# A slab opening with five tiles, a norm multiply moved to VectorE, and the order of the last waits

## The chip, the cores and the metric

The kernel runs on one core of a Trainium2 chip. The metric is the device time of one launch in microseconds (us). Several launches are timed and the median is taken.

## What is computed

The reference chains a linear attention and a feed-forward layer. Batch is 8, with 8 heads, 576 positions and a head dimension of 64; the layer is 512 to 2048 to 512.

```
q_s = softmax(q, over the head dimension)
k_s = softmax(k, over the sequence)
kv  = k_s^T v                      # 64 x 64 per batch and head
x   = q_s kv                       # laid out as 4608 tokens x 512
h   = x @ w_in                     # 4608 x 2048
g   = h * sigmoid(beta * h)
out = g @ w_out                    # 4608 x 512, float32
```

## The kernel before, in words

The output is made in nine slabs. Slab t (0 to 7) holds the first 512 positions of batch t; slab 8 holds the 64 positions that each batch has left over. The work on TensorE (PE) is one long list of matmuls:

- The **first pass** of a slab makes 16 tiles of 128 hidden features (function `pass1_mm`, L406 in the profile through the helper `mm`). A tile takes four matmuls of 512 columns, one for each part m of the 512 inputs (XT parts 0 to 3), summed in a bank of PSUM. ScalarE (ACT) then applies Silu (L746) and VectorE (DVE) scales the result (L769) into GT. The banks are HB (0, 1, 2) in turn; the fourth tile takes bank 3. The first three tiles are opened together, m by m, in the order of `LEAD`, so that XT parts 2 and 3 are wanted only after six matmuls.
- The **second pass** (`pass2_fast`, L846) multiplies by w_out as seven products of 16 matmuls of 256 columns, in the manner of Strassen: it works on sums (GS1, GS2, WSUM) and on differences of halves of GT, which `g_diff` makes in place on VectorE (L812). The products use one HB bank and the two OB banks 3 and 4. Product four is copied out of bank 3 by ScalarE, product five out of bank 4 by ScalarE (`copy`, L882), and products six and seven are added to TS by VectorE (`last`, L894) into O2S. Product seven uses bank 4 again, so it waits for the copy of product five.
- The **attention** for the next batches is laid between these matmuls. ScalarE takes the exponentials (L319). `norm_main` normalises q: VectorE sums (reduce L357) and inverts (L359), and then a multiply in place (L361) follows, for half a batch (two head pairs, 128x1024) on GpSimd (POOL). `turn` transposes that half by a DMA from SyncE's (SP) queue (L606) into QT. `kv_all` makes keys times values on PE (L482); VectorE scales it into KVD (L490, L459). `quad` multiplies KVD by QT on PE (L554); VectorE casts the even parts to XT and ScalarE the odd ones (L596). For slabs 2 and 3, part 0 and 1 (first half) are made late in the second pass before, part 2 and 3 (second half) within the opening of the slab itself. `cast_v` and `cast_vr` put v into bf16 on GpSimd (L377, L391).

The order is written out by hand in two ways. `tick` counts slots of PE (64 in a first pass, 64 in a second) and runs an entry of `todo` when its slot comes; `hooks` run at named places of the second pass (hook 3 ahead of product four, 4 ahead of five, 5 ahead of six, 6 ahead of seven). Each engine has one queue, in the order in which the program adds its instructions. Waits are put in by `Program.plan` from what an instruction reads and writes; `after` adds a further one.

`silu_table` is a tiny Silu activation (L1054) that makes ScalarE load the Silu table before it is wanted. `load` issues the loads of a batch from SP (three of 1 MB, for even batches four of the remaining rows as well). `store` sends a finished slab out from SP. At the end SP waits for all stores (L151).

Second pass t below is that of slab t: in second pass 1 the attention of batch 2 is made, in second pass 2 that of batch 3, and the exponentials of q of batch 4 as well.

Of the kernel before, what the change touches and what calls it, by code (L numbers as in the profile page):

```python
# [18 lines left out]
NF = DFF // 128  # L19
NM = DM // 128  # L20
NG = NF // 2
# [23 lines left out]
class Program:  # L45
# [83 lines left out]
    def emit(self, nc, es):  # L129
        counts, waits = self.plan()  # L130
        sems = {}
        for key in counts:
            sems[key] = es.enter_context(nc.semaphore("s_" + "_".join(str(x) for x in key)))
        by = {e: [] for e in (PE, ACTE, DVE, POOL, SP)}
        for op, w in zip(self.ops, waits):
            by[op.eng].append((op, w))

        def run(eng):
            def body(h):
                for op, w in by[eng]:  # L140
                    for key, n in w:
                        h.wait_ge(sems[key], n)
                    ins = op.fn(h)
                    if op.slot is not None:
                        ins.then_inc(sems[op.count[0]], 16)
                    elif op.inc:
                        ins.then_inc(sems[op.count[0]], 1)
                if eng == SP:
                    for key, n in sorted(counts.items(), key=str):
                        if key[0] == "dma" and str(key[1]).startswith("out"):  # L150
                            h.wait_ge(sems[key], n)  # L151
            return body

        with nc.Block() as blk:
            for e in (PE, ACTE, DVE, POOL, SP):
                getattr(blk, e)(run(e))


def bass_efficient_attn_shen__then__act_swish_beta_kernel(
# [12 lines left out]
    with ExitStack() as es:  # L172
# [48 lines left out]
        HB = (0, 1, 2)  # L221
        OB = (3, 4)
        MB = (5, 6, 7)

        P = Program()
# [376 lines left out]
        def turn(b, hp0, n):  # L602
            i = b % 2
            o = bass.AP(QT[i], hp0 * 512, [[2048, 128], [128, 4 * n], [1, 128]])
            a = bass.AP(EQ[i], hp0 * 512, [[2048, 128], [1, 512 * n]])
            add(SP, lambda e: e.dma_start_transpose(o, a),  # L606
                r=[("eq", i, hp) for hp in range(hp0, hp0 + n)],
                w=[("qt", i, hp) for hp in range(hp0, hp0 + n)], slot=f"tq{i}{hp0}")
# [6 lines left out]
        def norm_turn(b, hp0):  # L615
            norm_main(b, hp0, 2, POOL)
            turn(b, hp0, 2)

        def norm_turn_rem():
            norm_rem()  # L620
            turn_rem()

        def one(fn, *a):
            return lambda: fn(*a)

        def steps(fn, *a):
            return lambda: go(fn(*a))
# [8 lines left out]
        def attn_late(b):  # L636
            if b < 4:
                x = 100 if b == 2 else 97
                return [(x, steps(kv_all, b)), (x + .1, lambda: g_diff(1)),
                        (118, one(quad, b, (0,)))]  # L640
            return [(96, steps(kv_all, b)), (99, lambda: g_diff(1)), (112, one(quad, b))]

# [95 lines left out]
        hrot = [0]  # L738
# [16 lines left out]
                pass1_mm(t, f, m, bk)  # L755
                tick()

        LEAD = tuple((n, m) for m in range(NM) for n in range(3))

        def pass1_lead(t, fs, tick):  # L760
            bks = [HB[(hrot[0] + n) % 3] for n in range(3)]
            hrot[0] += 3
            for n, m in LEAD:
                pass1_mm(t, fs[n], m, bks[n])
                tick()

# [43 lines left out]
        def g_diff(fh):  # L810
            f, th = NG * fh, 1 - fh
            add(DVE, lambda e: e.tensor_tensor(gv(f, th, NG), gv(f, th, NG), gv(f, 1 - th, NG),  # L812
                                               ALU.subtract),
                r=gk(f, 0, NG) + gk(f, 1, NG), w=gk(f, th, NG), war=True)
# [140 lines left out]
        for t in range(NSLAB):  # L955
            todo = []
            if t == 0:
                todo = [(x, steps(t_steps, 1, (hp,), NOW, ACTE))
                        for hp, x in enumerate((97, 106, 114, 119))]
                todo += [(107, one(exp_kr_s, 1))]  # L960
                todo += [(x, one(exp_k, 1, hp, 1)) for hp, x in enumerate((108, 115, 120, 125.5))]
                todo += [(x, one(cast_v, 1, hp, DVE))
                         for hp, x in ((1, 118.5), (2, 123), (3, 127))]
                todo += [(x, steps(kv_steps, 1, (hp,), NOW))
                         for hp, x in enumerate((118, 122, 126))]
                todo += [(x, steps(out_step, 1, hp, NOW, ACTE)) for hp, x in enumerate((122.5, 125))]
                todo += [(117, one(o2_evac, 0, 0, 3, ACTE))]
                todo += [(2, steps(out_step, 0, 3, HEAD, DVE))]
            elif t < 4:
                todo = attn_late(t + 1)  # L970
                if t > 1:
                    todo += [(1.5, one(quad, t, (1,)))]
                if t == 3:
                    todo += [(4, one(norm_turn, 4, 2))]
                if t == 1:
                    todo += [(1, steps(out_step, 1, 2, (3,), ACTE)),
                             (3, steps(kv_steps, 1, (3,), (7,))),
                             (6, steps(out_step, 1, 3, (7,), DVE)),
                             (6.1, one(w_sum, 2, 4, 4)), (6.2, one(w_diff, 0)),
                             (6.3, one(w_diff, 1))]  # L980
            elif t < 7:
                todo = attn(t + 1)
            elif t == 7:
                todo = spread(outr_steps(1), 32, 48)
            todo = sorted(todo, key=lambda x: -x[0])
# [7 lines left out]
            def ftile(n):  # L993
                return n if t == 0 else n // 2 + NG * (n % 2)

            for n in range(NF + 1):
                if n == 0:
                    pass1_lead(t, [ftile(x) for x in range(3)], tick)
                elif 2 < n < NF:
                    pass1_tile(t, ftile(n), tick, 3 if n == 3 else None)  # L1000
                if n:
                    scale_g(ftile(n - 1))
                    for i_, w_ in {8: ((0, 4),), 12: ((4, 2),), 14: ((6, 1),), 16: ((7, 1),)}.get(
                            n if t else 0, ()):
                        g_sum1(i_, w_)
                        g_sum2(i_, w_)
                    if t == 2 and n == 2:
                        for hp in range(NHP):
                            cast_v(3, hp, after=P.writer[("gt", 0, 0)])
                if t == 0 and n == 14:  # L1010
                    w_sum(1)
                if t == 1 and n in (4, 7, 10):
                    o2_evac(0, n // 3, 3 + n // 3, ACTE)
                    if n == 10:
                        store(0)
# [28 lines left out]
            def on(n, fn, *a):  # L1044
                hooks.setdefault(n, []).append(lambda: fn(*a))
# [8 lines left out]
                add(ACTE, lambda e: e.activation(DUMMY[:, 2:3], WARM[:, 0:1], ACT.Silu),  # L1054
                    r=["warm"], w=["dummy"])

            def casts(b):
                g = P.writer[("gs2", NG - 1)]
                if b % 2 == 0:
                    cast_vr(b, after=g)  # L1060
                for hp in range(NHP):
                    cast_v(b, hp, after=g)

            if t == 1:
                on(0, exps, 2)
                on(0, casts, 2)
                on(2, norm_turn, 2, 0)
                on(3, norm_turn, 2, 2)
                on(3, g_diff, 0)
                on(4, silu_table)  # L1070
                on(3, load, 4)
            elif t == 2:
                on(0, exps, 3)
                on(2, norm_turn, 3, 0)
                on(3, norm_turn, 3, 2)
                on(3, g_diff, 0)
                on(3, load, 5)
                on(4, exp_q, 4)
                on(4, silu_table)
                on(4, casts, 4)  # L1080
                on(6, norm_turn, 4, 0)
            elif t == 3:
                on(0, exp_k, 4)
                on(0, exp_kr, 4)
                on(0, exp_q, 5)
                on(3, g_diff, 0)
                on(4, norm_turn, 5, 0)
                on(5, norm_turn, 5, 2)
                on(4, exp_qr, 1)
                on(5, exp_k, 5)  # L1090
                on(5, norm_turn_rem)
                on(5, casts, 5)
                on(5, load, 6)
                on(7, load_rem, "qrf", qt_h, QRF, 4)
            elif t + 2 < B:
                b = t + 2
                on(0, exps, b)
                on(0, casts, b)
                if t == 4:
                    on(0, load, 7)  # L1100
                on(3, norm_turn, b, 0)
                on(4, norm_turn, b, 2)
# [40 lines left out]
```

The softmax here doesn't subtract the row's maximum and nothing guards it: scores larger than these inputs give would overflow.

## Time and profile before

| What | Value |
|---|---|
| Median of 8 runs | 272.96 us (272.35 to 274.28) |
| The profiled execution | 272.75 us, of which span 270.9 us |
| TensorE matmuls | busy 264.1 us (97%), granted clock 0.998 |
| VectorE | busy 192.5 us (71%) |
| ScalarE | busy 181.3 us (67%) |
| GpSimd | busy 63.0 us (23%) |
| Second pass 1, slab 2 first pass | 60.65 to 74.67, 74.67 to 89.11 us |
| Second pass 2, slab 3 first pass | 89.11 to 103.69, 103.69 to 118.12 us |

The span is the time between the first and the last instruction in the profile; the rest of the execution's time lies around it. A matmul's record is longer than the distance to the next one, since they are pipelined: the start of a 512-column matmul comes 0.216 us after that of the one before it, the start of a 256-column one 0.109 us. In the profile's lines "DVE", "ACT", "POOL" and "SP" are VectorE, ScalarE, GpSimd and SyncE; "PEld" is TensorE's load of weights, and a "q" after a name is the engine's own queue of instructions, as for DMAs that it issues. A timeline line has the start, the duration, the engine, the line of code, the operation, its output and input, how many there were in a row, and in brackets the idle time before and what ended it.

### The profile page before, as it was taken

Reading aid. Unit: us, or ns where it says so; the run is one execution under the profiler, and the core shown is the slowest. Engines: PE = TensorE matmul, PEld = TensorE weight load, DVE = VectorE, ACT = ScalarE, POOL = GpSimd, SP = SyncE. Lnnn points to the kernel's source line nnn. Section 1 sums busy time; section 2 is a strip of 40 time slices with the busy share of each in tenths; the row PEclk is TensorE's granted clock in tenths of the full one; section 3 lists DMA queues with packets and bytes.
Section 4 is the critical chain, followed back from the end, with each engine's and each line's share of the span. In section 5 each row is a group of like instructions: output and inputs, shape, how many; then the busy total and the mean of one; then the engine's idle time right before and its main releaser. Section 6 shows DMA issues by size and latency. Waiting matters only on the chain.

```text
span 270.9 us, 5010 instructions
## 1 busy us (share of the span) xinstructions
PE 264.1 (97%) x1993; PEld 163.6 (60%) x1993; DVE 192.5 (71%) x407; ACT 181.3 (67%) x289; POOL 63.0 (23%) x80
## 2 busy tenths in 40 slices
PE   8999999999999999999999999999999999999994
PEld 2444444448744875478645864587458745874683
DVE  4964586887967798868778876887588448626762
ACT  4898658789468974887778937893883387018610
POOL 2790010006530089000910660036000100000000
PEclk9999999999999999999999999999999999999999
DMA  7999999989799129940499999503600130012005
GB/s 216 320 204 207 226 324 349 297 222 374 179 329 302 64 53 293 279 156 2 80 284 275 287 354 154 163 8 73 213 2 0 41 135 2 0 70 87 0 2 156
DMA packets 59367, 45.95 MB, mean 170 GB/s; under 512 B 28608, under 2 KB 58320, under 8 KB 58320
## 3 DMA queue, kind: packets, MB, share of 16 engines
q1 hardware_dynamic: 54480, 40.90, 53.7%
q0 software_dynamic: 4240, 4.19, 9.4%
q10 hardware_dynamic: 624, 0.53, 0.6%
q8 instruction: 16, 0.26, 0.4%
q14 instruction: 7, 0.06, 0.1%
HBM read 36.71 MB, written 9.44 MB: 170 GB/s over the span
## 4 chain that ended last, share of the span: by engine, by line
PE 84%; DVE 4%; DMA 3%; ACT 2%; POOL 2%; SPq 2%; issue 1%; POOLq 0%
PE PS L406 50%; PE PS L846 31%; DMA VF<-in_v_dram 2%; PE PS L482 1%; PE PS L554 1%; DMA QT<-EQ 1%; POOL VB L377 1%; DVE QS L357 1%; SPq L278 1%; SPq L290 1%; ACT EQ L319 1%; DVE EQ L361 1%; POOL EQ L361 1%; DVE VB L377 1%; ACT GT L746 1%
## 5 line engine op out<-in xcount | busy, mean ns | idle before, releaser
L406 PE MATMUL PS<-XT,WIN 128*128 128x512 bf16 x576 | 127.8, 380 | 0.1
L746 ACT ACTIVATE GT<-PS,BETA 128x512 bf16<-128x512 f32 x144 | 95.2, 689 | 39.5 <-PE PS L406 39.3
L406 PEld LDWEIGHTS PS<-XT,WIN 128*128 128x128 bf16 x576 | 55.0, 98 | 64.8 <-DVE XT L596 0.7
L769 DVE TENSOR_SCALAR GT<-GT,RB 128x512 bf16<-128x512 bf16 x144 | 52.5, 386 | 38.7 <-ACT GT L746 37.9
L361 POOL TENSOR_TENSOR EQ<-EQ,QI 128x1024 bf16<-128x1024 bf16 (+1 forms) x13 | 25.6, 1966 | 48.8 <-DVE QI L359 48.1
L846 PE MATMUL PS<-WSUM,GT 128*128 128x256 bf16 x256 | 30.1, 273 | 1.0 <-ACT O2S L882 1.0
L846 PE MATMUL PS<-WOUT,GS 128*128 128x256 bf16 x256 | 31.1, 273 | 0.0
L846 PE MATMUL PS<-WOUT,GT 128*128 128x256 bf16 x256 | 29.8, 273 | 0.0
L846 PEld LDWEIGHTS PS<-WSUM,GT 128*128 128x128 bf16 x256 | 24.8, 98 | 5.0 <-ACT O2S L882 1.2
L882 ACT COPY O2S<-PS 128x512 f32<-128x512 f32 (+1 forms) x17 | 9.4, 559 | 26.1 <-PE PS L846 26.1
L846 PEld LDWEIGHTS PS<-WOUT,GT 128*128 128x128 bf16 x256 | 24.8, 98 | 3.0
L846 PEld LDWEIGHTS PS<-WOUT,GS 128*128 128x128 bf16 x256 | 24.8, 98 | 3.0
L319 ACT ACTIVATE EQ<-QF 128x512 bf16<-128x512 f32 x32 | 17.9, 620 | 7.4 <-DMA QF<-in_q_dram 7.3
L805 DVE TENSOR_TENSOR GS<-GT 128x512 bf16<-128x512 bf16 (+2 forms) x32 | 21.9, 685 | 0.0
L812 DVE TENSOR_TENSOR GT<-GT 128x2048 bf16<-128x2048 bf16 x16 | 21.6, 1374 | 0.0
L377 POOL CAST VB<-VF 128x512 bf16<-128x512 f32 x24 | 15.6, 650 | 22.1 <-DVE GS L805 13.4
L357 DVE TENSOR_REDUCE QS<-EQ 128x16 f32<-128x1024 bf16 (+1 forms) x20 | 19.7, 984 | 0.9 <-ACT EQ L319 0.9
L319 ACT ACTIVATE EK<-KF 128x512 bf16<-128x512 f32 x32 | 18.1, 620 | 0.1
L894 DVE TENSOR_TENSOR O2S<-TS,PS 128x512 f32<-128x512 f32 (+1 forms) x17 | 10.8, 647 | 9.7 <-PE PS L846 9.7
L846 PE MATMUL PS<-WSUM,GS 128*128 128x256 bf16 x128 | 16.6, 273 | 0.0
L406 PE MATMUL PS<-WOUT,GT 128*128 128x512 bf16 x64 | 15.5, 380 | 0.0
L846 PEld LDWEIGHTS PS<-WSUM,GS 128*128 128x128 bf16 x128 | 12.5, 98 | 3.2
(90 smaller groups left out, 209.4 us busy)
## 6 DMA issues: line engine op xcount, KB each, us to landing
out_dram<-O2S SPq DMA_DIRECT2D x8, 1024.0 KB, 4.9
QF<-in_q_dram SPq DMA_DIRECT2D x6, 1024.0 KB, 7.0
KF<-in_k_dram SPq DMA_DIRECT2D x6, 1024.0 KB, 9.4
VF<-in_v_dram SPq DMA_DIRECT2D x6, 1024.0 KB, 12.2
KF<-in_k_dram SPq DMA_DIRECT2D x8, 256.0 KB, 5.5
VF<-in_v_dram SPq DMA_DIRECT2D x8, 256.0 KB, 5.5
WOUT<-in_moe_w_out_dram POOLq DMA_DIRECT2D x4, 512.0 KB, 16.4
WIN<-in_moe_w_in_dram POOLq DMA_DIRECT2D x3, 512.0 KB, 9.1
```

The source lines that it names most:

```text
L319: add(ACTE, lambda e, o=o, a=a: e.activation(o, a, ACT.Exp), r=[(name + "f", i, hp)], w=[("e" + name, i, hp)])
L357: add(DVE, lambda e: e.tensor_reduce(s_, a, AX.X, ALU.add), r=ks, w=[("qs", i, hp0)])
L361: add(eng, lambda e: e.tensor_tensor(a, a, vb, ALU.mult), r=ks + [("qi", i, hp0)], w=ks)
L377: add(eng, lambda e: (e.copy if eng == ACTE else e.tensor_copy)(o, a), r=[("vf", i, hp), ("vone", i)], w=[("vb", i, hp)], after=after)
L406: add(PE, lambda e: e.matmul(o, l, r_, start=start, stop=stop), r=r, w=w, bank=[bk])
L746: add(ACTE, lambda e: e.activation(GT[:, f, :], PS[bk][:, :], ACT.Silu, scale=BETA[:, f:f + 1]), r=[("ps", bk), "beta"], w=[("gt", f, 0), ...
L769: add(DVE, lambda e: e.tensor_scalar(GT[:, f, :], GT[:, f, :], RB[:, f:f + 1], None, ALU.mult), r=k + ["rb"], w=k)
L805: add(DVE, lambda e: e.tensor_tensor(GS2[:, i:i + n, :], GT[:, i:i + n, :], GT[:, i + NG:i + NG + n, :], ALU.add), r=[k_ for f in (i, i + ...
L812: add(DVE, lambda e: e.tensor_tensor(gv(f, th, NG), gv(f, th, NG), gv(f, 1 - th, NG), ALU.subtract), r=gk(f, 0, NG) + gk(f, 1, NG), w=gk(f ...
L846: add(PE, lambda e, l=l, r_=r_, st=st, u=u, i=i, b_=b_: e.matmul(PS[b_][:, 256 * u:256 * u + 256], l, r_, start=st, stop=end and i == NG - ...
L882: add(eng, lambda e, b_=b_, u0=u0, u1=u1: (e.copy if eng == ACTE else e.tensor_copy)(o[:, u0:u1, :], bank3(b_)[:, u0:u1, :]), r=[("ps", b_ ...
L894: add(DVE, lambda e, b_=b_, u0=u0, u1=u1: e.tensor_tensor(o[:, u0:u1, :], ts[:, u0:u1, :], bank3(b_)[:, u0:u1, :], ALU.add), r=["ts", ("ps ...
```

## The change

Three things are changed.

1. Slabs 2 and 3 open with five tiles m by m instead of three. The fourth and fifth use the OB banks 3 and 4. Their order is m = 0 and 1 of four tiles, m = 0 and 1 of the fifth, then m = 2 and 3 of all five: parts 2 and 3 of XT are wanted after ten matmuls. The quad that makes these parts goes from tick 1.5 to tick 6.
2. For batches 2 and 3 the sums and inverses of the second half stay at hook 3, but the multiply goes from GpSimd to VectorE, after keys times values and the second difference; its transpose follows it. The difference and the multiply are one entry of `todo` (`diff_norm`). The loads of batches 4 and 5 go from hook 3 to hook 4, the casts of batch 4 wait for that multiply, and in second pass 2 the Silu table goes from hook 4 to hook 6.
3. At the end SP waits for the stores in the order of their issue instead of the order of their names.

```diff
+        last = {op.count[0]: op.pos for op in self.ops if op.slot is not None}
...
-                    for key, n in sorted(counts.items(), key=str):
-                        if key[0] == "dma" and str(key[1]).startswith("out"):
-                            h.wait_ge(sems[key], n)
+                    for key in sorted((k for k in counts if str(k[1]).startswith("out")),
+                                      key=lambda k: last[k]):
+                        h.wait_ge(sems[key], counts[key])
...
+        def diff_norm(b):
+            g_diff(1)
+            norm_main(b, 2, 2, sums=False)
+            turn(b, 2, 2)
...
-                return [(x, steps(kv_all, b)), (x + .1, lambda: g_diff(1)),
+                return [(x, steps(kv_all, b)), (x + .1, one(diff_norm, b)),
                         (118, one(quad, b, (0,)))]
...
-        LEAD = tuple((n, m) for m in range(NM) for n in range(3))
+        LEAD = {3: tuple((n, m) for m in range(NM) for n in range(3)),
+                5: tuple([(n, m) for m in range(2) for n in range(4)] + [(4, 0), (4, 1)]
+                         + [(n, m) for m in range(2, NM) for n in range(5)])}
 
         def pass1_lead(t, fs, tick):
-            bks = [HB[(hrot[0] + n) % 3] for n in range(3)]
+            bks = [HB[(hrot[0] + n) % 3] for n in range(3)] + list(OB)
             hrot[0] += 3
-            for n, m in LEAD:
+            for n, m in LEAD[len(fs)]:
...
-                    todo += [(1.5, one(quad, t, (1,)))]
+                    todo += [(6, one(quad, t, (1,)))]
                 if t == 3:
                     todo += [(4, one(norm_turn, 4, 2))]
...
+            lead = 5 if t in (2, 3) else 3
             for n in range(NF + 1):
                 if n == 0:
-                    pass1_lead(t, [ftile(x) for x in range(3)], tick)
-                elif 2 < n < NF:
+                    pass1_lead(t, [ftile(x) for x in range(lead)], tick)
+                elif lead <= n < NF:
...
+            def norm_sums(b, hp0):
+                norm_main(b, hp0, 2, mult=False)
+
-            def casts(b):
-                g = P.writer[("gs2", NG - 1)]
+            def casts(b, key=("gs2", NG - 1)):
+                g = P.writer[key]
...
             if t == 1:
...
-                on(3, norm_turn, 2, 2)
+                on(3, norm_sums, 2, 2)
                 on(3, g_diff, 0)
                 on(4, silu_table)
-                on(3, load, 4)
+                on(4, load, 4)
             elif t == 2:
...
-                on(3, norm_turn, 3, 2)
+                on(3, norm_sums, 3, 2)
                 on(3, g_diff, 0)
-                on(3, load, 5)
                 on(4, exp_q, 4)
-                on(4, silu_table)
-                on(4, casts, 4)
+                on(4, casts, 4, ("eq", 1, 2))
+                on(4, load, 5)
+                on(6, silu_table)
                 on(6, norm_turn, 4, 0)
```

## The prediction

> **What bounds the kernel now.** I read the busy shares first, then the chain that ended last, then the timeline of the two stretches that the diff touches, engine by engine, and last the waits.
>
> ```profile
> PE 264.1 (97%) x1993; PEld 163.6 (60%) x1993; DVE 192.5 (71%) x407; ACT 181.3 (67%) x289; POOL 63.0 (23%) x80
> PE 84%; DVE 4%; DMA 3%; ACT 2%; POOL 2%; SPq 2%; issue 1%; POOLq 0%
> ```
>
> TensorE is busy in 97% of the span and carries 84% of the chain. So an edit pays or costs what it adds to, or takes from, TensorE's idle gaps. The gaps lie at the end of second passes 1 and 2 and where slabs 2 and 3 open:
>
> ```profile
> 70.66 2.12 DVE L812 TENSOR_TENSOR GT<-GT 128x2048 bf16<-128x2048 bf16 x1
> 72.28 0.41 PE L554 MATMUL PS<-QT,KVD 64*64 64x512 bf16 x4 [0.24 <-DMA QT<-EQ]
> 72.62 2.21 PE L846 MATMUL PS<-WSUM,GT 128*128 128x256 bf16 x17
> 74.67 0.60 PE L406 MATMUL PS<-XT,WIN 128*128 128x512 bf16 x2
> 75.19 0.41 PE L554 MATMUL PS<-QT,KVD 64*64 64x512 bf16 x4
> ...
> 98.95 2.12 DVE L812 TENSOR_TENSOR GT<-GT 128x2048 bf16<-128x2048 bf16 x1
> 99.90 1.28 ACT L1054 ACT_TABLE_LOAD   x1
> 100.31 0.41 PE L554 MATMUL PS<-QT,KVD 64*64 64x512 bf16 x4
> 100.65 0.28 PE L846 MATMUL PS<-WSUM,GT 128*128 128x256 bf16 x1
> 101.31 0.57 ACT L882 COPY O2S<-PS 128x512 f32<-128x512 f32 x1
> 101.93 0.28 PE L846 MATMUL PS<-WSUM,GT 128*128 128x256 bf16 x1 [0.99 <-ACT O2S L882]
> 102.19 1.20 DVE L357 TENSOR_REDUCE QS<-EQ 128x16 f32<-128x1024 bf16 x1
> 103.89 0.69 DVE L894 TENSOR_TENSOR O2S<-TS,PS 128x512 f32<-128x512 f32 x1 [0.21 <-PE PS L846]
> ```
>
> In second pass 2 the largest single gap shows: the last product's first matmul starts at 101.93 instead of 100.76 (100.65 plus one 256-column step of 0.109), because ScalarE's copy of its bank stands behind a table load. Slabs 2 and 3 themselves have almost no gap: from 75.54 on, matmuls follow every 0.216 us. And the last lines of the span:
>
> ```profile
> SPq L151 <- DMA out_dram<-O2S: 1.9, 1, 1.9
> L151 SPq EVENT_SEMAPHORE  x6: 17/28/1872, 268.3 to 270.5; - x6
> ```
>
> SyncE's second of six waits takes 1.87 us and ends at 270.26, when the last output has landed; the other four follow, 0.06 us apart, before the closing barrier.
>
> [...] this same multiply (L361 on DVE) takes 0.691 us. [...] the two L812 instructions above take 2.12 us beside GpSimd's multiply and 1.22 elsewhere, and GpSimd's second multiply takes 2.76 instead of 1.90. [...] The trace has the 1.28, but the next activation starts 1.29 after it, so I charge 1.28 alone.
>
> **The change, part by part.** Times are those of the profile before, without the shift that earlier parts bring.
>
> *Second pass 1 and slab 2.* One GpSimd multiply (2.76) goes. The second difference then is free of it: 1.22, ending at 71.88 instead of 72.78. The last product, which reads its output and started at 72.93, starts when TensorE is ready, at 72.73: **-0.20**. The slab opens at 74.47. The new DVE multiply starts at 71.80 (two L812 in a row start 1.135 apart) and ends at 73.02. What is queued behind it on DVE, the cast of XT part 0 and the two O2S sums, moves by 0.25; XT part 0 is done at 73.7, and bank 3, which the fourth tile now opens, is free at 74.3, both in time. The transpose is issued at 73.05 instead of 71.72; the one before landed 3.18 after its issue, so it lands at 76.22. TensorE comes to the quad after six matmuls, 74.47+6x0.216, plus 0.09 for its loads: 75.86. It can start at 76.27, a new wait of **+0.41**. (Before, it came after two, at 75.19, and the data were there at 74.90.) XT part 2 is cast behind the quad with four matmuls between, as before: nothing.
>
> *Five tiles.* Their last matmuls end 0.216 us apart, so five Silus stand in a row; consecutive Silus start 0.57 apart and take 0.69 (77.49, 78.07, 78.64, 79.21, 79.78 in this trace). Tile 5 takes the first tile's bank: it wants it 5x0.216 = 1.08 after the first tile's last matmul started, and gets it 0.417 (matmul to Silu) + 0.688 + 0.056 = 1.16 after: 0.08. Tile 8 takes tile 5's bank, wants it at 17x0.216+0.08 = 3.75, and gets it at 0.417+2.86+0.70+0.056 = 4.03: 0.28. Tile 9 has slack. Together **+0.36** in slab 2 and **+0.36** in slab 3. Before, three tiles and one on bank 3 left these waits out. Bounds: 0 if Silus in a row start every 0.51, 0.8 if every 0.65.
>
> *Second pass 2.* The table load and its dummy (1.28+0.20) go behind the copy of the last product's bank and the cast of XT part 1. That copy starts when the four Exps end, 99.91, and is done at 100.49; the difference is done at 100.17; so the last product starts at 100.76: **-1.17**. The table load then runs from 101.35 to 102.85, and ScalarE's next work, the cast of XT part 3, comes after 104: hidden.
>
> *Slab 3.* It opens at 102.52. The DVE multiply runs from 100.09 to 101.31, the transpose goes at 101.34 instead of 100.01 and lands 3.17 later, 104.50; TensorE is at the quad at 103.90 and starts it at 104.55: **+0.65**. Then XT part 2. DVE behind the multiply: cast of part 0 at 101.28, O2S sum 101.88, reduce of batch 4's first half 102.48, reciprocal 103.72, O2S sum 103.89. Next in its queue is no longer the cast of part 2: batch 4's second statistics are put in at tick 4, the quad now at tick 6, so a reduce (start 104.49, 1.24 to the next) and a reciprocal (105.73) go first. The cast runs from 105.90 to 106.59. TensorE wants it at 104.55+1.22 = 105.77, gets it at 106.65: **+0.88**.
>
> *Moved off the path.* Each multiply that moves adds 1.22 to DVE. Six GpSimd casts of batch 4 now wait for it: they start at 101.4 instead of 100.1, and the two multiplies of batch 4 behind them end at about 109.4 instead of 109.0; their transposes land by 119, and the quad of batch 4 is at 128.2. Load 4 (three main DMAs, then four remainder DMAs and a store behind it on SP) and load 5 (three) were already behind the transpose on SP; they go 1.35 later. QF of batch 4, issued at 73.0, has a median landing of 7.0 and is read at 97.7; that of batch 5, issued at 101.3, is read at 122.8. If that cover were gone, each would cost its 1.35.
>
> *Tail.* With waits in order of issue, the last to land is the last to be waited for. Four waits of 0.06 no longer follow it: **-0.24** (0 if the waits are paired differently by the compiler).
>
> Sum: -0.20+0.41+0.36-1.17+0.65+0.88+0.36-0.24 = **+1.05 us**. The profiled execution took 272.75 (span 270.9, 1.85 around it), 0.21 under the median of 272.96. So 273.8 by its own time, **274.0** by the median. Unknown sizes: the DVE multiply from 0.96 (0.69 and the step that the all-bf16 sums L805 take from 512 to 1024, 0.42 to 0.68) to 1.38 (twice 0.69) moves each of the three waits behind it by -0.26 to +0.16, together -0.8 to +0.5.
>
> **Rivals.**
> *No slower (273.1).* One mechanism: the reduce of batch 4 in slab 3 does not hold the cast of XT part 2. Price 0.88, leaving +0.2. It decides if DVE reaches the cast before 105.0, that is if its queue runs 0.9 ahead of my count. For it: before, DVE had 0.21 idle there. Against it: all instructions from 98.95 on stand back to back. With the Silu rows absorbed as well (-0.72) it becomes 272.4, still inside 0.3%.
> *Much slower (275.5).* The transposes land later than 3.2 after issue. Landings reach 8.3 in the trace, where loads fill the queue, and other ones of this kernel take 3 to 4.8 to issue instead of 1.24. Half of such a delay, 1.5 us in one slab, would do. Against it: the next loads still stand behind these transposes on SP.
> *The reorder on ScalarE does not do what it says (275.2).* If the copy still waits, as it must stand behind four Exps, -1.17 is lost. The Exps end at 99.89, so TensorE needs 0.27 of slack to vanish first.
> *Faster by over 0.3% (271.7).* All new waits gone, [...] with half the Silu term. It would need the transposes to land 0.65 sooner after a later issue, and the DVE queue to be short as well.
>
> **How the numbers follow.** About 0.3%, 0.82 us, is what a measurement of this kernel can tell from no change. My sum is +1.05, with some 0.7 of uncertainty from multiply, Silu rows and waits: slower by over 0.3% 0.66 (forecast 0.50, transposes late 0.10, copy still late 0.06), within 0.3% 0.28 (the no-slower rival, and the forecast with small terms), faster 0.06. Range 272.7 to 275.2: from between the two no-slower figures, to the lost ScalarE gain.
>
> **What would show it.** Right: L812 at 1.22 in all of second passes 1 and 2; L361 on DVE with two 128x1024 instructions near 1.22; no ScalarE wait of 0.99 before the last product; waits for QT of 0.4 and 0.65 at the two quads; a wait of 0.9 for L596 after the second; 0.3 of TensorE gap before tile 8. Wrong: no gap at the part-2 matmuls of slab 3, or quads that start without a wait.

## The result, and the profile after

The changed kernel takes 274.21 us (median of 11 runs, 273.40 to 275.61), the kernel before 272.85 us (32 runs). The ratio is 1.0054, with a 95% interval of 1.0037 to 1.0072: slower by 0.54%, or some 1.4 us. (Here and below a ratio is an estimate from all runs and not the quotient of the two medians, which differ by 1.36 us here.) In the slower runs the granted clock tends to be lower: three of the four slowest of the changed kernel had 0.995 to 0.997 and the others 0.998 to 1.000, and of the six runs of the experiment with three tiles and the late quad the three slowest had 0.994 and the other three 1.000. The profiled execution took 274.25 us, its span 272.4, against 272.75 and 270.9 before: +1.50.

The stages show where it went. Windows of the kernel before, then of the changed one: second pass 1, first pass of slab 2, second pass 2, first pass of slab 3 (length, and then busy time and number of instructions of each engine, granted clock, DMA share and GB/s). Each window begins with the first matmul of its pass; for second passes 2 and 3 of the kernel before that is 88.94 and 117.96, and not 89.11 and 118.12 as the table above has it.

```profile
60.65:74.67 14.02, 13.76 (x158) 11.62 (x156) 11.40 (x20) 10.02 (x17) 8.33 (x8) 1.00 0.91 276
74.67:88.94 14.27, 14.27 (x70) 6.21 (x68) 10.43 (x22) 10.43 (x16) 2.45 (x4) 1.00 1.08 324
88.94:103.69 14.75, 13.76 (x158) 11.61 (x157) 12.66 (x22) 11.38 (x20) 7.91 (x6) 1.00 0.26 55
103.69:117.96 14.27, 14.27 (x71) 6.18 (x68) 11.84 (x24) 10.43 (x16) 5.03 (x5) 1.00 1.10 315
```

```profile
60.73:74.56 13.83, 13.60 (x157) 11.62 (x156) 11.57 (x21) 10.03 (x17) 5.57 (x7) 1.00 0.82 257
74.56:90.17 15.61, 14.62 (x71) 6.04 (x69) 10.36 (x22) 10.08 (x16) 2.45 (x4) 1.00 1.09 285
90.17:103.76 13.59, 13.59 (x157) 11.60 (x156) 11.54 (x22) 11.06 (x19) 2.84 (x3) 1.00 0.19 56
103.76:119.75 15.99, 14.77 (x70) 6.04 (x68) 12.12 (x26) 10.49 (x18) 6.52 (x7) 1.00 1.08 306
```

The two second passes became shorter by 0.19 and 1.16 us. The two first passes became longer by 1.34 and 1.72. Second pass 1 begins 0.08 later. From second pass 3 to the end the changed kernel needs 152.70 us instead of 152.99, and 0.22 of that is the tail below: the loads and casts that were moved cost nothing there. The timeline of TensorE in the changed kernel names the waits:

```profile
72.70 2.03 PE L854 MATMUL PS<-WSUM,GT 128*128 128x256 bf16 x17
74.56 1.46 PE L407 MATMUL PS<-XT,WIN 128*128 128x512 bf16 x6
76.89 0.41 PE L555 MATMUL PS<-QT,KVD 64*64 64x512 bf16 x4 [0.87 <-DMA QT<-EQ]
...
101.90 2.03 PE L854 MATMUL PS<-WSUM,GT 128*128 128x256 bf16 x17
103.76 1.46 PE L407 MATMUL PS<-XT,WIN 128*128 128x512 bf16 x6
105.78 0.41 PE L555 MATMUL PS<-QT,KVD 64*64 64x512 bf16 x4 [0.56 <-DMA QT<-EQ]
106.13 1.04 PE L407 MATMUL PS<-XT,WIN 128*128 128x512 bf16 x4
107.70 0.61 PE L407 MATMUL PS<-XT,WIN 128*128 128x512 bf16 x2 [0.54 <-DVE XT L597]
```

Both last products now run through: the 17 matmuls in one piece are the last one of product six and the 16 of product seven (before, product seven waited 0.20 us in second pass 1 and 1.17 in second pass 2). Both quads wait for QT, and behind slab 3's quad the fifth matmul waits for the cast of XT part 2. An idle time in brackets counts from the modelled end of the matmul before, which overlaps the next; I therefore give waits from start to start, less the usual step (0.216 us for 512 columns, 0.109 for 256): 1.03 and 0.73 at the quads (0.09 of each was there before), 0.70 at the cast. VectorE in second pass 2 and slab 3:

```profile
100.18 1.22 DVE L820 TENSOR_TENSOR GT<-GT 128x2048 bf16<-128x2048 bf16 x1
101.31 1.22 DVE L362 TENSOR_TENSOR EQ<-EQ,QI 128x1024 bf16<-128x1024 bf16 x1
...
105.61 1.21 DVE L358 TENSOR_REDUCE QS<-EQ 128x16 f32<-128x1024 bf16 x1
106.85 0.25 DVE L360 RECIPROCAL QI<-QS 128x16 f32<-128x16 f32 x1
107.02 0.63 DVE L597 CAST XT<-PS 128x512 bf16<-128x512 f32 x1
```

The difference takes 1.22 where it took 2.12, and the moved multiply takes 1.22. The reduce and reciprocal of batch 4 stand ahead of the cast, though the quad's first results were there when the reduce was still running. At the end of the span, SyncE waits for the stores:

```profile
SPq L152 <- DMA out_dram<-O2S: 1.5, 5, 0.6
L152 SPq EVENT_SEMAPHORE  x6: 17/28/28, 270.7 to 272.0; - x6
```

Five waits end with a landing each, 0.6 us at most. The last output lands at 271.96, and the last instruction ends 0.49 later; before, it was 0.71.

### The profile page after: what moved, and what is told of

It reads as the page before. It is cut to its first block, busy times and chain, and to the rows that moved or that the text cites. A ratio compares the mean times of both kernels' runs of the same rounds, so it can differ in the third digit from the quotient of the medians.

```text
span 272.4 us, 5008 instructions
## 1 busy us (share of the span) xinstructions
PE 264.7 (97%) x1993; PEld 163.2 (60%) x1993; DVE 192.1 (71%) x409; ACT 180.8 (66%) x289; POOL 56.4 (21%) x78
## 4 chain that ended last, share of the span: by engine, by line
PE 77%; DVE 9%; DMA 5%; ACT 3%; POOL 2%; SPq 2%; issue 1%; POOLq 0%; DVEq 0%
PE PS L407 46%; PE PS L854 28%; ACT GT L752 3%; DMA QT<-EQ 3%; DVE QS L358 3%; DMA VF<-in_v_dram 2%; PE PS L555 1%; DVE EQ L362 1%; PE PS L483 1%; POOL VB L378 1%; DVE GT L820 1%; SPq L279 1%; SPq L291 1%; POOL EQ L362 1%; DVE QI L360 1%
## 5 line engine op out<-in xcount | busy, mean ns | idle before, releaser
L777 DVE TENSOR_SCALAR GT<-GT,RB 128x512 bf16<-128x512 bf16 x144 | 51.8, 380 | 39.9 <-ACT GT L752 39.1
L362 POOL TENSOR_TENSOR EQ<-EQ,QI 128x1024 bf16<-128x1024 bf16 (+1 forms) x11 | 20.0, 1822 | 47.8 <-DVE QI L360 47.3
L820 DVE TENSOR_TENSOR GT<-GT 128x2048 bf16<-128x2048 bf16 x16 | 19.9, 1268 | 0.0
```

The source lines that it names most:

```text
L362: add(eng, lambda e: e.tensor_tensor(a, a, vb, ALU.mult), r=ks + [("qi", i, hp0)], w=ks)
L777: add(DVE, lambda e: e.tensor_scalar(GT[:, f, :], GT[:, f, :], RB[:, f:f + 1], None, ALU.mult), r=k + ["rb"], w=k)
```

## The experiments

The theory is the sum of the prediction: separate waits on TensorE, each with its own releaser. Its main rivals are that waits hide one another, or that a wait has another releaser. All times below are medians; the kernel before, run beside them, had 272.88 to 272.95.

**The order of the last waits alone**, put into the kernel before.

```diff
...
-                    for key, n in sorted(counts.items(), key=str):
...
+                    for key in sorted((k for k in counts if str(k[1]).startswith("out")),
+                                      key=lambda k: last[k]):
...
```

> Kernel before with the third part alone: SyncE awaits the stores in the order of issue. Theory (each satisfied wait behind the last landing costs 0.06 us, four go): 0.24 us shorter, so 272.6 against 272.85, and from the landing of the last output to the end of the span 0.42 instead of 0.66 us. Rival (the waits are paired so that as many still follow): no difference, still 0.66 us.

272.65 against 272.95, ratio 0.9989 (0.9974 to 1.0003). The interval takes in no change, so the runs alone don't show the gain. The profile does: from the last landing to the last instruction 0.48 instead of 0.71. (The expectation's 0.66 and 0.42 counted to the start of the last instruction and not to its end; the difference is the same.)

**The table load alone**, put into the kernel before.

```diff
                 on(4, exp_q, 4)
-                on(4, silu_table)
                 on(4, casts, 4)
+                on(6, silu_table)
```

> Kernel before with the Silu table of second pass 2 at hook 6 instead of hook 4, and nothing else. Theory: the 1.17 us gap before the last product of second pass 2 goes, but about half comes back where slab 3 opens: the quad now comes earlier than its transpose (wait 0.2), and VectorE's statistics of batch 4, put in ahead of the last O2S sum, hold the cast of XT part 2 (wait 0.5). Net -0.5 us, 272.4. Rival 1 (nothing comes back): -1.17 us, 271.7. Rival 2 (the copy still waits for ScalarE): 0, 272.85.

272.32 against 272.95, ratio 0.9974 (0.9964 to 0.9983). The net is what was expected, but not in its parts. TensorE and VectorE in this run:

```profile
98.74 2.12 DVE L812 TENSOR_TENSOR GT<-GT 128x2048 bf16<-128x2048 bf16 x1
100.44 0.28 PE L846 MATMUL PS<-WSUM,GT 128*128 128x256 bf16 x1
101.00 1.91 PE L846 MATMUL PS<-WSUM,GT 128*128 128x256 bf16 x16 [0.27 <-DVE GT L812]
```

The copy is out of the way, and the next releaser shows: the second difference, which here, with the multiply on GpSimd, still takes 2.12 us (1.22 in the changed kernel, where the multiply is on VectorE). Of the 1.17 us gap 0.44 stays. So the table load by itself is worth 0.72, and the other 0.44 belongs to the multiply's move; the experiment that puts the multiply back on GpSimd has the same 0.44 again. Little came back: the slab opened so much later than I had counted that the cast held TensorE by 0.18 only, and the quad not at all.

**Batch 4's statistics behind the quad**, in the changed kernel.

```diff
-                    todo += [(4, one(norm_turn, 4, 2))]
+                    todo += [(7, one(norm_turn, 4, 2))]
```

> Changed kernel, but the statistics and multiply of batch 4's second half are put in at tick 7 of slab 3 instead of tick 4, that is behind the quad and its casts. Theory (VectorE's queue holds the cast of XT part 2 by one reduce and one reciprocal): the 0.70 us wait between the fourth and fifth matmul after slab 3's quad goes, the rest stays: 0.7 us under the changed kernel, about 273.5. Rival (the cast is late because of its bank or the quad): the wait stays, same time as the changed kernel, 274.2.

273.61, ratio to before 1.0018 (1.0005 to 1.0031); the changed kernel has 1.0054. The wait is gone:

```profile
106.81 0.41 PE L555 MATMUL PS<-QT,KVD 64*64 64x512 bf16 x4 [0.54 <-DMA QT<-EQ]
107.15 5.89 PE L407 MATMUL PS<-XT,WIN 128*128 128x512 bf16 x26
```

After the quad 26 matmuls follow without idle time that the profile counts. The theory stands, and the medians differ by 0.60 where 0.7 was expected. The profiled execution itself took 274.58 and so no less than the changed kernel's 274.25: in it both transposes of batch 2 landed late (after 3.91 and 4.63 us), and the two quads that need them waited 0.96 and 1.37.

**Tiles 8 and 9 on banks 3 and 4**, in the changed kernel.

```diff
-                    pass1_tile(t, ftile(n), tick, 3 if n == 3 else None)
+                    pass1_tile(t, ftile(n), tick, 3 if n == 3 else OB[n - 8] if lead == 5 and n in (8, 9)
+                               else None)
```

> Changed kernel, but in slabs 2 and 3 tiles 8 and 9 take banks 3 and 4 again instead of the HB bank of tile 5 and 6. Theory (five Silus in a row keep tile 5's bank 0.28 us too long): the 0.28 us gap before tile 8 goes in both slabs, the 0.08 us before tile 5 stays: 0.57 us under the changed kernel, about 273.6. Rival (ScalarE is behind whatever the bank): a gap of 0.2 to 0.3 us shows up a few tiles later, and the time is that of the changed kernel, 274.2.

273.75, ratio 1.0020 (1.0005 to 1.0036). In the changed kernel the matmuls' starts show 0.29 before tile 8 and 0.08 before tile 5 in both slabs. Here the first is gone in both and none opens later in the slab; the second stays. In the timeline these gaps are too short for brackets, but the same 39 matmuls behind slab 2's quad take 9.00 us in the changed kernel and 8.70 here:

```profile
77.23 9.00 PE L407 MATMUL PS<-XT,WIN 128*128 128x512 bf16 x39
...
77.61 8.70 PE L407 MATMUL PS<-XT,WIN 128*128 128x512 bf16 x39
```

So it was the bank and not ScalarE's backlog.

**The multiply back on GpSimd**, with all else as changed.

```diff
         def diff_norm(b):
             g_diff(1)
-            norm_main(b, 2, 2, sums=False)
-            turn(b, 2, 2)
...
-                on(3, norm_sums, 2, 2)
+                on(3, norm_turn, 2, 2)
...
-                on(3, norm_sums, 3, 2)
+                on(3, norm_turn, 3, 2)
```

> Changed kernel with the multiply and transpose of the second half of batches 2 and 3 put back on GpSimd at hook 3; five tiles, quad at tick 6, loads, table and waits stay as changed. Theory (what the move buys is the 0.2 us of the second difference in second pass 1, what it costs is the late transpose): both quads start without a wait for QT (-1.03 and -0.73 us), the difference takes 2.12 us again (+0.2), and in slab 3 the cast of XT part 2, which VectorE's queue sets, is only about 0.3 us earlier, so that its wait grows from 0.7 to about 1.2 us (+0.5). Net -1.0 us, about 273.2. Rival [...]: not faster than the changed kernel.

273.46 against 272.90, ratio 1.0021 (1.0012 to 1.0030), so 0.75 under the changed kernel's median. Both quads run without a wait for QT, as expected. The gap before the last product came back twice (0.40 and 0.45, for the difference), and the cast of XT part 2 holds 0.68:

```profile
101.65 1.91 PE L852 MATMUL PS<-WSUM,GT 128*128 128x256 bf16 x16 [0.27 <-DVE GT L818]
103.61 1.24 PE L407 MATMUL PS<-XT,WIN 128*128 128x512 bf16 x5
104.78 0.41 PE L555 MATMUL PS<-QT,KVD 64*64 64x512 bf16 x4
105.13 1.04 PE L407 MATMUL PS<-XT,WIN 128*128 128x512 bf16 x4
106.67 0.61 PE L407 MATMUL PS<-XT,WIN 128*128 128x512 bf16 x2 [0.51 <-DVE XT L597]
```

The move buys 0.85 at the two products and costs 1.57 at the two quads. The expectation had missed the gap in second pass 2, and the wait for the cast did not grow from 0.70 to about 1.2, as it said.

**Instruction fetches shifted**, in the changed kernel.

```diff
         warm(10, 0)
+        for _ in range(15):
+            mm(PS[0][:, 0:128], WARM[:, 0:128], WARM[:, 0:128], True, True, r=["warm"],
+               w=[("ps", 0)], bk=0)
```

> Changed kernel with 15 more warming matmuls of 128 columns at the start[...]. In the changed kernel's profile the second transpose of batch 2 took 2.44 us to issue and 3.73 to land, beside a 16 KB fetch at 73.86 to 75.09 us. Theory [...]: the issue takes 1.24 and the landing 3.2 us after it, the wait before slab 2's quad falls from 1.03 to about 0.45 us; the start gets up to 0.9 us longer from the added matmuls. Rival (the transpose is slow for another reason): issue, landing and wait stay as they were.

273.99, ratio 1.0054 (1.0036 to 1.0072): the total doesn't tell it from the changed kernel. The transpose does. With the added matmuls the fetch of instructions (q8 in the lines below) began at 72.93 us instead of 73.86, while the issue of the transpose came at 72.72 instead of 73.12. In the changed kernel, DMA traffic from 72.5 to 77.5 us, 40 slices of 0.125:

```profile
GB/s 0 0 0 0 0 0 0 0 0 0 131 0 0 0 70 209 211 201 199 119 31 8 6 10 10 12 43 279 289 291 112 0 0 0 41 33 123 115 25 172
q8 instruction: 1, 0.02, 1.5%
QT<-EQ SPq DMA_TRANSPOSE x1, 3.7
```

and with the fetch earlier, from 72.4 to 78.5 us, slices of about 0.15:

```profile
GB/s 0 0 0 107 0 0 0 0 0 13 173 217 215 196 69 151 289 285 108 3 0 7 54 60 34 13 282 275 195 255 302 356 342 389 389 376 410 369 376 363
q8 instruction: 1, 0.02, 1.0%
QT<-EQ SPq DMA_TRANSPOSE x1, 3.1
```

In the first, the fetch (the lone 131; 73.86 to 75.08) overlaps the transpose, whose packets run at some 200 GB/s. They then nearly stop for about 0.7 us, 75.1 to 75.8, which is behind the end of the fetch, and go on. In the stop 6 to 12 GB/s are left; what holds the packets back is not shown. In the second, the fetch (107; 72.93 to 73.95) ends as the packets of the transpose begin. The transpose lands 3.10 after its issue instead of 3.73, and the wait before the quad is 0.61 instead of 1.03. The issue, though, took 1.74 and not 1.24: in that the expectation was wrong. The start did not get visibly longer.

**Three tiles with the late quad**, in the changed kernel.

```diff
-            lead = 5 if t in (2, 3) else 3
+            lead = 3
```

> Changed kernel with slabs 2 and 3 opened by three tiles again, quad still at tick 6. Theory: XT part 2 is wanted right behind the quad, so four matmuls (0.86 us) of cover go in each slab, and the Silu rows (0.37 us in each) go too: +1.7 -0.7, net about +1.0 us, 275.2. Rival (the five tiles cost more than they cover): at or under the changed kernel, 274.2 or less.

275.97 (six runs, 274.38 to 277.45), ratio 1.0114 (1.0080 to 1.0147). The cast of XT part 2 now stands right behind the quads, for 0.88 us more than in the changed kernel in slab 2 and 0.91 in slab 3, and the Silu gaps are gone. By these gaps it is +1.05, about the expected +1.0; the profiled executions differ by 1.47. The rest lies ahead of the edit: second pass 1 begins at 61.34 instead of 60.73, and its quad waits 0.20 less. The medians differ by 1.76, but the six runs scatter over 3 us, so 1.76 is not the size of the effect.

**Both mends in the changed kernel**: the edits of the third and fourth experiment together.

> Changed kernel with both mends at once: statistics of batch 4's second half at tick 7, and tiles 8 and 9 of slabs 2 and 3 on banks 3 and 4. Theory (the two waits are separate terms of one sum on TensorE): 0.70 + 0.57 = 1.27 us under the changed kernel, about 272.9, the time of the kernel before. Rival (one hides the other): no better than the better of the two alone, 273.6.

272.96 against 272.88, ratio 1.0005 (0.9990 to 1.0021). The two add up: 1.25 under the changed kernel for the expected 1.27. In this profile, with no shift made, the fetch fell at 73.36 to 74.24, and the transpose landed after 3.12.

**A version from the parts that pay.** Kernel before, with the last waits in order, the table at hook 6, and both statistics of batch 4 behind slab 3's quad.

```diff
-                    todo += [(4, one(norm_turn, 4, 2))]
+                    todo += [(7, one(norm_turn, 4, 0)), (8, one(norm_turn, 4, 2))]
...
-                on(6, norm_turn, 4, 0)
```

> Kernel before (multiply on GpSimd, three tiles) with the waits in order of issue, the Silu table of second pass 2 at hook 6, and both statistics of batch 4 moved behind slab 3's quad (ticks 7 and 8). Theory: -0.24 from the waits, -1.17 from the table, and only some 0.2 us comes back (the quad's transpose), since nothing of batch 4 is ahead of the cast of XT part 2: 1.2 us under the kernel before, about 271.65. Rival (the gap reopens elsewhere, through later scales or transposes of batch 4): 272.4 or more.

271.92 against 272.90, ratio 0.9968 (0.9956 to 0.9981). Nothing of batch 4 holds the cast, and the quad doesn't wait either. But the difference held the last product by 0.44 here too; that is what the expectation missed.

**The second difference in two halves**, added to that.

```diff
-        def g_diff(fh):
-            f, th = NG * fh, 1 - fh
...
+        def g_diff(fh, cuts=1):
+            th, n = 1 - fh, NG // cuts
+            for f in range(NG * fh, NG * fh + NG, n):
...
-                return [(x, steps(kv_all, b)), (x + .1, lambda: g_diff(1)),
+                return [(x, steps(kv_all, b)), (x + .1, lambda: g_diff(1, 2)),
```

> The version with the multiply on GpSimd, three tiles, table at hook 6, waits in order and batch 4's statistics behind the quad, which still had a gap of 0.44 us before the last product of second pass 2; now the second difference of second passes 1 and 2 is two instructions of 128x1024 instead of one of 128x2048. Theory (the gap is the difference, held by GpSimd's multiply until 100.0 us, and the last product needs only its first half to start): the 0.44 us gap goes, and up to 0.4 us in second pass 1 where the quad does not hide it: about 271.4. Rival (the last product waits for something else): gap and time stay, 271.9.

271.80 against 272.88, ratio 0.9951 (0.9934 to 0.9968).

```profile
99.43 2.60 DVE L814 TENSOR_TENSOR GT<-GT 128x1024 bf16<-128x1024 bf16 x2
101.14 2.03 PE L848 MATMUL PS<-WSUM,GT 128*128 128x256 bf16 x17
```

The last product runs in one piece while VectorE is still at the second half, although the two halves take 2.60 us where the one instruction took 2.12. Some of it came back: the quads in the slabs now wait 0.30 and 0.21 for QT. With only six runs, from 270.92 to 272.33, the step from 271.92 is not shown by the medians.

**The first quad three ticks later**, added to that.

```diff
-                        (118, one(quad, b, (0,)))]
+                        (121, one(quad, b, (0,)))]
```

> The same, and the quad of the first half of batches 2 and 3 goes from tick 118 to tick 121 of the second pass before (five or six 256-column matmuls later). Theory: in second pass 1 TensorE waited 0.2 to 0.7 us for that transpose; with 0.57 us more cover 0.2 to 0.6 us goes, and the casts of XT parts 0 and 1 still end before the slab opens: about 271.0. Rival (the casts now come too late for the slab's first matmuls): no gain or a loss, 271.4 or more.

271.67 (five runs), ratio 0.9957 (0.9945 to 0.9969): not to be told from the one before. The waits of the quads are gone, but the last product, which now begins ahead of the first quad, comes too early for the difference:

```profile
98.83 1.91 PE L848 MATMUL PS<-WSUM,GT 128*128 128x256 bf16 x16
100.98 0.60 PE L848 MATMUL PS<-WSUM,GT 128*128 128x256 bf16 x4 [0.23 <-DVE GT L814]
```

It starts 0.40 late in both second passes. The rival was right that there is no gain, but for another reason than it gave: the casts were in time.

## Why the prediction was right

The forecast was 274.0 us and slower; 274.21 was measured. Its sum was +1.05, and the same terms read from the profile after give +1.4; the profiled executions differ by 1.50. The path was right: every new wait that was forecast is there, with the releaser that was named. That the total fits to 0.2 us is in part luck: one term was 0.53 too small and another 0.18 too large, and the kernel before came out 0.11 lower with more runs. Term by term:

| Term | Predicted | Measured |
|---|---|---|
| Second pass 1: difference free of GpSimd | -0.20 | -0.20 |
| Slab 2: quad waits for QT | +0.41 | +0.94 |
| Slab 2: Silu rows | +0.36 | +0.37 |
| Second pass 2: last product | -1.17 | -1.17 |
| Slab 3: quad waits for QT | +0.65 | +0.63 |
| Slab 3: cast of XT part 2 behind batch 4 | +0.88 | +0.70 |
| Slab 3: Silu rows | +0.36 | +0.37 |
| Tail | -0.24 | -0.22 |

**The step that failed** is "so it lands at 76.22", in slab 2. The issue came as forecast (73.12 against 73.05), but the landing followed after 3.73 instead of the 3.18 of the transpose before. I took one landing for a constant. The shifted fetch and the other profiles point to the term that was missing: a 16 KB instruction fetch fell on the transfer, while the old, earlier transpose was nearly finished when the fetch began (74.18, landing 74.90). In the two profiles in which the fetch came early (instruction fetches shifted, and both mends) the same wait is 0.52 and 0.53, so the late landing accounts for some 0.4 of the 0.94.

**Right in sum, loosely attributed**: the -1.17. The prediction named both conditions (the copy at 100.49 and the difference at 100.17) but told of the gap as ScalarE's alone. Table load alone: 0.72; the rest needs the freed difference. My later expectations for the table alone and for the first combined version carried the mistake on.

**The cast**: 0.70 for 0.88. The order in the queue was right and removing it removed the wait; VectorE's instructions in the row stood 0.11 closer than I had added up, and the cast itself took 0.63 instead of 0.69.

**The multiply.** The prediction put it at 1.22 us on VectorE for 128x1024, and three of its terms rest on that. No row of before has this form; from the rows of before it could only be put between 0.96 and 1.38, so the 1.22 was an assumption of mine within these bounds. The profile after has 1.22 for both. **The Silu rows** (0.08 and 0.29) were as worked out.

Of the rivals, the late transposes came true in part: half a microsecond in one slab, and not 1.5. The rival that the reduce of batch 4 would not hold the cast was wrong, and so was the one that the reorder on ScalarE would not do what it says.

## What to carry to other kernels

Take a wait away only after asking which releaser is next in line: here a copy hid a difference, and once the copy was gone the difference held the same matmul by 0.44 of the 1.17 us. When an entry is moved within an order written by hand, look at what it is moved past on every engine: the quad went from tick 1.5 to 6, past a statistics entry at tick 4, and this cost 0.7 us on VectorE's queue that one number (tick 7) gave back. And where a long producer runs beside another engine's work and takes longer (the difference: 2.12 us with the multiply on GpSimd, 1.22 without), let the consumer start on half of it: two instructions of 128x1024 in place of one, 2.60 us together, removed a wait of 0.44 us that moving the multiply to VectorE removed only at the price of a later transpose. No gain in the total time was shown for it here.

## What the runs showed of the hardware that was not expected

In these profiles a transpose DMA beside a fetch of instructions (q8 in the profile: 16 of them with 0.26 MB, so 16 KB each) landed later. The second transpose of batch 2 was issued at 72.7 to 73.7 us in six profiles with the multiply on VectorE. Where the fetch began 0.2 to 0.4 us after its issue, it landed 3.10 and 3.12 after it (fetch at 72.93 and 73.36). Where the fetch began 0.5 to 1.3 us after the issue, it landed 3.55, 3.73, 4.24 and 4.63 after it (fetch at 74.19, 73.86, 73.97 and 74.57; they last 1.2 to 1.6 us). In these four the landing followed the end of the fetch by nearly the same time, 1.81, 1.77, 1.77 and 1.78 us: the later the fetch ended, the later the transpose landed. In the kernel before and the experiments with the multiply on GpSimd the fetch began 2.4 us after the issue or later, and the landing came after 3.14 to 3.34. The second transpose of batch 3, with no such fetch near it, took 3.14 to 3.18 in all six.

In the one run that was made to shift the fetch, the transpose landed 3.10 us after its issue instead of 3.73; by what way a fetch would delay a transpose these profiles don't show. A fetch is not the only thing beside which a transpose landed late. The first transpose of batch 2 had none while it ran, and it landed after 3.35, 3.65 and 3.91 us in three of the six and after 3.14 to 3.15 in the others. Packets of 8 KB of earlier transfers were on the way beside its own, three, four and eight of them in the late ones and one to three in the others; no experiment varied them.
